# A linear-attention and two-MoE kernel: one visit of each attention step to TensorE from the second block on, and another order inside the slots of the first

## The chip, the cores and the metric

The kernel runs on one core of a Trainium2 chip. The metric is the device time of one execution in microseconds (us). Five engines work side by side, each through its own queue in order: TensorE (PE in the views), VectorE (DVE), ScalarE (ACT), GpSimd (POOL) and SyncE (SP, which here only issues DMAs).

## The reference, cut to what matters

```python
def _attn_ref(q, k, v, f_logit):                 # (4, 8, 768, 48) each
    f = 1.0 / (1.0 + np.exp(-f_logit))
    for t in range(S):
        state = f[:, :, t, :, None] * state + np.einsum('bhd,bhe->bhde', k[:, :, t], v[:, :, t])
        y[:, :, t] = np.einsum('bhd,bhde->bhe', q[:, :, t], state)

x = attention output as (3072, 384)
x = (x @ w_a) * (x @ w_b) @ w_out                # d_ff 1536
h = x @ w_in ; x = (h - np.tanh(h)) @ w_out2     # d_ff 2048
```

## The kernel before

**The attention** is computed in 24 steps: 12 chunks of 64 positions, two batches to a step. Each step is a generator (`attn_step`) that yields between twelve phases, named by letters. F: ACT takes the sigmoid. P and R: DVE scans (tiles PRE and R). K: DVE makes KH and RA (L306, L307). V: ACT copies the running state ST into VS_A and VS_B. S: PE multiplies sc = KH by RA and transposes KH into pk. M: ACT copies RB from RA, then sc into RA and into RB, then pk into KTS (L326 to L333), and POOL masks RA and RB (affine_select, L329). U: PE makes uu from KTS, DVE adds the state into T1 (L348), POOL scales it back into ST. Y: PE makes yy, which reads RA, RB, VS_A and VS_B. E and L: ACT and DVE copy yy into two parts of x. D: DMAs bring a third of the heads into their places.

**The first MoE layer** follows in 6 blocks of 512 tokens, 4 attention steps each. A block has 12 rounds of three groups of nine 128x512 matmuls: a, b, y. Each group is one slot, so a block has 36 slots (`SLOTS`). After a, ACT copies it to asb; after b, DVE multiplies gf = asb times b, ACT makes gh, and gl is the difference (on POOL in block 0, later on DVE). y lags one round. Its sums stay in three PSUM banks for a whole block; after the last y, `store_x2` copies each bank with ACT into oh and subtracts with DVE into ol, and SP stores both. oh and ol have two buffers each for three banks. The steps 0 to 3 run ahead of block 0 by a list written out by hand (`SEQ`); later steps run during the block before the one that needs them. The table `pulses` says at which slot which phase is emitted: in block 0 by FIRST and OFF, later at 9 slots a step. S stands at slot 0 of the nine, U at 2, Y at 3, so a step comes to PE three times.

**The weights** arrive as 64-bit numbers. In block 0 each slot also makes one weight tile (`w_tick`): three DVE operations (cv, cv, wc, L125 to L127), a copy on ACT (L137), a subtraction on POOL (L139). A slot needs about the tile that was made four slots earlier. In block 0 the tick stands ahead of the slot's phases. Later blocks convert the second layer's weights, two tiles in nine slots.

**The second MoE layer** (h and o groups) runs from about 575 us to the end and is not touched.

The order on every queue is the order in which the program emits: `tc.manual_schedule()` moves nothing. `x2` buffers, PSUM banks and staging buffers come free by semaphores.

Of the kernel before, what the change touches and what calls it, by code (L numbers as in the profile page):

```python
# [18 lines left out]
CH = 64  # L19
# [9 lines left out]
def tile_kernel(ctx: ExitStack, tc: tile.TileContext, q, k, v, f, w_a, w_b, w_out, w_in, w_out2, l_fkq, l_tv, l_v, l_w1, l_w2, out):  # L29
    nc = tc.nc  # L30
# [21 lines left out]
    SLOTS = 3 * MF  # L52
    LEAD = 7
    FIRST = (-5, 4, 12, 20)
    PHASES = "FPRKVSMUYELD"
    OFF = (0, 1, 2, 4, 5, 7, 7, 9, 10, 10, 11, 12)
    CONV = (3, 7)
    SEQ = ("lf0 lk0 lf1 lt0 lk1 lv0 lf2 lt1 lv1 lk2 w lf3 lt2 lv2 lk3 w lt3 lv3 w x x x x F0 P0 F1 R0 K0 x x lf4 lk4 x V0 S0 P1 M0 F2 "
# [95 lines left out]
    def bank(i, name):  # L154
        return psp.tile([128, 512], F32, tag=f"b{i}", name=name)
# [3 lines left out]
    def att_bank(name):  # L159
        rot["att"] = (rot["att"] + 1) % rot["n"]  # L160
        return bank(rot["att"], name)

    def mm_split(dst, lhs, rhs, first, last):
        for i, (l_, r_) in enumerate(((lhs[0], rhs[0]), (lhs[0], rhs[1]), (lhs[1], rhs[0]))):
            nc.tensor.matmul(dst, l_, r_, start=(first and i == 0), stop=(last and i == 2))  # L165

    with tc.manual_schedule(), ExitStack() as p1:
# [8 lines left out]
        def gtile(tag, shape, name):  # L176
            bufs = {"gh": 4, "gl": 4, "oh": 2, "ol": 2, "asb": 1}[tag]
            n = 1
            for x in shape[1:]:
                n *= x  # L180
            w = TW if tag in ("gh", "gl") else 512
            t = gp.tile([128, w], F32, tag=tag, name=name, bufs=bufs)[:, :n]
            if len(shape) == 3:
                t = t.rearrange("p (u s) -> p u s", s=shape[2])
            return t

        class Work:
            def __init__(self, mk):
                self.F = mk("gh", [128, TW], "F")
                self.PRE = mk("gh", [128, NS], "PRE")  # L190
                self.R = mk("gl", [128, NS], "R")
                self.D2 = mk("gl", [128, NS], "D2")
                self.VS_A = mk("ol", [128, U, 64], "VS_A")
                self.VS_B = mk("ol", [128, U, 64], "VS_B")
                self.T1 = mk("asb", [128, U, D], "T1")
                self.KH = mk("gh", [128, U, CH], "KH")
                self.RA = mk("gh", [128, U, CH], "RA")
                self.RB = mk("gl", [128, U, CH], "RB")
                self.KTS = mk("gl", [128, 512], "KTS")
                self.F3 = self.F[:, 0:NS].rearrange("p (u s) -> p u s", s=SL)  # L200
                self.PRE3, self.R3, self.D23 = (
                    x.rearrange("p (u s) -> p u s", s=SL) for x in (self.PRE, self.R, self.D2))

        raw = {}
        for name in ("F", "D2", "R", "KH", "KTS", "PRE", "T1", "VX", "VX", "RA", "RB", "VS_A", "VS_B"):
            raw.setdefault(name, []).extend(wpool.tile([128, TW], F32, tag="w", name=name) for _ in range(PRO - 2))
# [12 lines left out]
        for i in range(PRO):  # L219
            work.append(Work((atile, gtile)[i] if i < 2 else wtile))  # L220
        VX = [[wtile("w", [128, 6, 64], "VX") for _ in range(2)] for _ in range(2)]
        VX = [[t.rearrange("p (b k) d -> p b k d", b=2) for t in s_] for s_ in VX]
# [33 lines left out]

        wdum = const.tile([128, 512], BF16, name="wdum")
        nc.vector.memset(wdum, 0.0)
# [23 lines left out]
        def attn_step(i):  # L282
# [19 lines left out]
            yield  # L302
            KH, RA, RB, KTS = w.KH, w.RA, w.RB, w.KTS
            k3 = tk.rearrange("p (u s) -> p u s", s=CH)
# [3 lines left out]
            yield  # L308
            if c > 0:
                nc.scalar.activation(VS_A[0:64, :, 0:D], st[0:64], ACTF.Copy)  # L310
                nc.scalar.activation(VS_B[64:128, :, 0:D], st[64:128], ACTF.Copy)
            if i < PRO:
                for vx, vs in zip(VX[i % 2], (VS_A, VS_B)):
                    nc.scalar.activation(
                        vx[:, :, :, 48:64], vs[:, U - 2:U, 0:D].rearrange("p b (k x) -> p b k x", x=16), ACTF.Copy)
            yield
            sc = att_bank("sc").rearrange("p (u s) -> p u s", s=CH)
            for u in range(U):
                nc.tensor.matmul(sc[64:128, u], KH[0:64, u], RA[0:64, u], start=True, stop=True)  # L319
                nc.tensor.matmul(sc[0:64, u], KH[64:128, u], RA[64:128, u], start=True, stop=True)  # L320
            pk = att_bank("pk")
            for j in range(NJ):
                nc.tensor.transpose(  # L323
                    pk[:, 128 * j:128 * (j + 1)], KH[:, 2 * j:2 * j + 2, :].rearrange("p u s -> p (u s)"), ident)
            yield
            nc.scalar.activation(RB[64:128], RA[64:128], ACTF.Copy)  # L326
            for r_, rows in ((RA, slice(64, 128)), (RB, slice(0, 64))):
# [4 lines left out]
                )  # L332
            nc.scalar.activation(KTS, pk, ACTF.Copy)  # L333
            yield
            uus = [att_bank(f"uu{bl}").rearrange("p (u s) -> p u s", s=CH) for bl in range(2)]
            for j in range(NJ):
# [15 lines left out]
            yield  # L352
            yy = att_bank("yy").rearrange("p (u s) -> p u s", s=CH)
            direct = jb == 0
# [45 lines left out]
        for jb in range(1, NBLK):  # L400
            for si in range(blocks[jb]):
                for p, o in enumerate(OFF):
                    at = FIRST[si] + o if jb == 1 else SLOTS * (jb - 1) + 9 * si - LEAD + o
                    pulses.append((at, first[jb] + si, p))
# [4 lines left out]
        def pulse(i, p):  # L409
            assert phase[i] == p  # L410
            phase[i] += 1
            if i >= PRO and p == 0 and i + 1 < NSTEP:
                load_t(i + 1, slice(0, 3))
            if i >= PRO and PHASES[p] == "K" and i + 1 < NSTEP:
                load_tv(i + 1)
            next(gens[i], None)
            if i >= PRO and PHASES[p] == "Y" and i + 1 < NSTEP:
                load_v(i + 1)
# [27 lines left out]
        def y_group(jb, m):  # L446
            n = 128 * blocks[jb]
            if m == 0:
                ys[jb] = [bank(5 + d, f"y{d}")[:, :n] for d in range(KT)]
            g = G.pop((jb, m))  # L450
            wo = W["o", m]
            for d in range(KT):
                cs = slice(128 * d, 128 * d + 128)
                mm_split(ys[jb][d], [w[:, cs] for w in wo], g, m == 0, m == MF - 1)
            if m == MF - 1:
                store_x2(jb, n)

# [16 lines left out]
        def moe1(prev):  # L474
            for jb in range(NBLK):
                n = 128 * blocks[jb]
                xx = [X[jb][:, hl].rearrange("p k s c -> p k (s c)")[:, :, :n] for hl in range(2)]
                for m in range(MF):
                    pab = []
                    for bi, nm in enumerate("ab"):  # L480
# [6 lines left out]
                        if nm == "a":  # L487
                            asb = gp.tile([128, 512], F32, tag="asb", name="asb", bufs=1)[:, :n]
                            nc.scalar.activation(asb, pb, ACTF.Copy)  # L489
                            yield jb  # L490
                    gf = gp.tile([128, 512], F32, tag="gf", name="gf", bufs=1)[:, :n]
                    gh = gp.tile([128, TW], F32R, tag="gh", name="gh", bufs=4)[:, :n]
# [15 lines left out]
        for it in SEQ.split():  # L508
            if it == "c":
                w_tick(nconv[0] + 1)  # L510
            elif it == "w":
                w_fetch(len(loaded) + 1)
            elif it == "x":
                warm()
            elif it[0] == "l":
                i = int(it[2])
                if it[1] == "f":
                    load_t(i, slice(0, 1))
                elif it[1] == "k":
                    load_t(i, slice(1, 3))  # L520
                else:
                    (load_tv if it[1] == "t" else load_v)(i)
            else:
                i, p = int(it[1]), PHASES.index(it[0])
                if i >= PRO:
                    pulses.pop(0)
                pulse(i, p)
        for i in range(PRO):
            pulse(i, len(PHASES) - 1)
        npro = nconv[0]  # L530
# [13 lines left out]
        for g, jb in enumerate(moe1(None)):  # L544
            slot = g % SLOTS
            if jb == 0:
                w_tick(min(NW1, npro + slot + 1))
            else:
                if g == SLOTS:
                    rot.update(n=3, conv=None)  # L550
                if spilled:
                    w_spill()
                if (g + LEAD) % (SLOTS // 4) in CONV and jb < NBLK - 1 or (jb == NBLK - 1 and slot == 0):
                    w_tick(min(nconv[0] + 1, NW2 + 1))
# [249 lines left out]
```

## Time and profile before

| | |
|---|---|
| median of 3 runs | 980.62 us (980.6 to 981.83) |
| the profiled execution | 981.35 us, span 979.4 us |
| PE busy | 952.7 us, 97% of the span |
| DVE busy | 605.5 us, 62% |
| ACT busy | 491.4 us, 50% |
| POOL busy | 133.4 us, 14% |

The span runs from the first to the last instruction; the execution's own time is 1.95 us longer and 0.73 us above the median. Matmuls overlap, and their ends are modelled, so the distance from one start to the next tells more than a busy share. The views give in brackets how long an instruction's engine sat idle before it and what ended that.

### The profile page before, as it was taken

The page shows a single profiled execution, that of the slowest core. Times are in us where ns is not written, and L with a number is a line of the kernel's source. Part 1 is how long each engine was busy: PE and PEld are TensorE (multiplying, and loading weights), DVE is VectorE, ACT ScalarE, POOL GpSimd, SP SyncE. Part 2 cuts the span into 40 slices and gives each one's busy share as a digit, 9 for nine tenths or more (in the row PEclk, how much of TensorE's full clock was granted, in tenths as well). Part 3 has the DMA queues.
Part 4 walks back from the last instruction along what each step waited for, and adds up shares of the span by engine and source line. Part 5 has one row for each costly group of instructions (what it writes and reads, how often), then busy time and mean ns, then how long its engine had stood idle before and what let it go on. Part 6 is the DMA issues. An engine that isn't in the chain of part 4 may idle for free.

```text
span 979.4 us, 15868 instructions
## 1 busy us (share of the span) xinstructions
PE 952.7 (97%) x6155; PEld 766.7 (78%) x6155; DVE 605.5 (62%) x1021; ACT 491.4 (50%) x949; POOL 133.4 (14%) x144
## 2 busy tenths in 40 slices
PE   7898899999999999999999999999999999999997
PEld 5677777878888878877888888888888888888885
DVE  6988866556666665565442257666666666666663
ACT  5544544344433444443321156666666666666663
POOL 6566651111111111111000000000000000000000
PEclk9999999999999999999999999999999999999999
DMA  9566656445534643472248650100100100200001
GB/s 284 134 185 172 185 125 192 113 108 179 145 108 125 195 124 109 141 196 85 76 159 291 192 180 1 63 35 1 65 33 1 65 33 16 82 0 1 33 1 35
DMA packets 41171, 104.53 MB, mean 107 GB/s; under 512 B 5600, under 2 KB 8672, under 8 KB 41088
## 3 DMA queue, kind: packets, MB, share of 16 engines
q1 hardware_dynamic: 40368, 102.45, 35.3%
q10 hardware_dynamic: 720, 0.98, 0.5%
q8 instruction: 50, 0.82, 0.4%
q14 instruction: 33, 0.27, 0.1%
HBM read 74.71 MB, written 26.74 MB: 104 GB/s over the span
## 4 chain that ended last, share of the span: by engine, by line
PE 88%; DVE 6%; issue 2%; ACT 2%; DMA 1%; SPq 0%; POOL 0%; DVEq 0%; ACTq 0%
PE o L165 20%; PE h L165 20%; PE b L165 14%; PE a L165 13%; PE y L165 13%; PE yy L358 2%; PE sc L319 2%; DVE cv L126 2%; PE uu L340 1%; DVE cv L125 1%; PE pk L323 1%; DVE wc L127 1%; DMA VS_B<-in_l_v_dram 1%; DVE R L299 1%; DVE gf L494 0%
## 5 line engine op out<-in xcount | busy, mean ns | idle before, releaser
L165 PE MATMUL h<-x,w_i 128*128 128x512 f32 x864 | 212.6, 391 | 0.0
L165 PE MATMUL o<-gh,w_p 128*128 128x512 f32 x576 | 195.1, 394 | 0.0
L165 PEld LDWEIGHTS h<-x,w_i 128*128 128x128 f32 x864 | 162.2, 188 | 36.1
L165 PE MATMUL a<-x,w_a 128*128 128x512 f32 x648 | 163.9, 397 | 2.6 <-ACT asb L489 2.3
L165 PE MATMUL b<-x,w_b 128*128 128x512 f32 x648 | 164.4, 398 | 0.0
L165 PE MATMUL y<-gh,w_o 128*128 128x512 f32 x432 | 148.0, 397 | 0.0
L165 PEld LDWEIGHTS a<-x,w_a 128*128 128x128 f32 x648 | 120.3, 188 | 30.4 <-ACT asb L489 2.7
L165 PEld LDWEIGHTS b<-x,w_b 128*128 128x128 f32 x648 | 119.9, 189 | 25.3
L105 DVE SCALAR_TENSOR_TENSOR xu<-u,h 128x512 f32<-128x512 f32 x96 | 66.0, 688 | 111.4 <-ACT u L102 111.2
L494 DVE TENSOR_TENSOR gf<-asb,b 128x512 f32<-128x512 f32 x72 | 49.3, 685 | 137.2 <-PE b L165 84.6
L165 PEld LDWEIGHTS o<-gh,w_p 128*128 128x128 f32 x576 | 108.1, 188 | 25.0 <-issue 0.2
L102 ACT ACTIVATE u<-h 128x512 f32<-128x512 f32 x96 | 57.4, 598 | 132.6 <-PE h L165 131.9
L165 PE MATMUL o<-gl,w_p 128*128 128x512 f32 x288 | 112.9, 392 | 0.0
L495 ACT ACTIVATE gh<-gf 128x512 fp32r<-128x512 f32 x72 | 45.5, 632 | 130.7 <-DVE gf L494 130.6
L489 ACT ACTIVATE asb<-a 128x512 f32<-128x512 f32 x72 | 42.9, 596 | 132.1 <-PE a L165 130.5
L165 PEld LDWEIGHTS y<-gh,w_o 128*128 128x128 f32 x432 | 81.8, 189 | 18.9
L165 PE MATMUL y<-gl,w_o 128*128 128x512 f32 x216 | 85.4, 395 | 0.0
L107 DVE SCALAR_TENSOR_TENSOR v<-v,v 128x512 f32<-128x512 f32 x96 | 66.5, 693 | 10.3 <-ACT gh L575 0.5
L106 DVE SCALAR_TENSOR_TENSOR v<-v,xu 128x512 f32<-128x512 f32 x96 | 66.5, 692 | 10.3 <-ACT v L103 0.5
L103 ACT ACTIVATE v<-u,bias 128x512 f32<-128x512 f32 x96 | 69.5, 724 | 3.1
L104 ACT ACTIVATE v<-u,bias 128x512 f32<-128x512 f32 x96 | 68.1, 709 | 0.6 <-DVE gl L576 0.6
L576 DVE TENSOR_TENSOR gl<-v,gh 128x512 fp32r<-128x512 f32 x96 | 65.7, 685 | 0.2 <-ACT gh L575 0.2
(95 smaller groups left out, 1114.4 us busy)
## 6 DMA issues: line engine op xcount, KB each, us to landing
wst<-in_l_w_dram SPq DMA_DIRECT2D x68, 384.0 KB, 3.3
wsp<-wst SPq DMA_DIRECT2D x32, 384.0 KB, 2.6
T<-in_l_fkq_dram SPq DMA_DIRECT2D x38, 288.0 KB, 5.4
x<-xs SPq DMA_DIRECT2D x12, 768.0 KB, 5.2
w_i<-wsp SPq DMA_DIRECT2D x16, 384.0 KB, 3.5
w_p<-wsp SPq DMA_DIRECT2D x16, 384.0 KB, 3.5
TV<-in_l_tv_dram SPq DMA_DIRECT2D x24, 192.0 KB, 2.8
xs<-oh SPq DMA_DIRECT2D x18, 256.0 KB, 2.3
```

The costliest lines, as they stand in the source:

```text
L102: nc.scalar.activation(u, h, ACTF.Square, accum_out=total)
L103: nc.scalar.activation(v1, u, ACTF.Square, bias=bias1)
L104: nc.scalar.activation(v2, u, ACTF.Square, bias=bias2)
L105: nc.vector.scalar_tensor_tensor(xu, u, Q4, h, ALU.mult, ALU.mult)
L106: nc.vector.scalar_tensor_tensor(v1, v1, Q_Y1, xu, ALU.add, ALU.mult)
L107: nc.vector.scalar_tensor_tensor(v2, v2, Q_Y2, v1, ALU.add, ALU.mult)
L126: nc.vector.scalar_tensor_tensor(t, hi, -1073741824, t, ALU.bitwise_and, ALU.bitwise_or)
L165: nc.tensor.matmul(dst, l_, r_, start=(first and i == 0), stop=(last and i == 2))
L489: nc.scalar.activation(asb, pb, ACTF.Copy)
L494: nc.vector.tensor_tensor(gf, asb, pab[1], ALU.mult)
L495: nc.scalar.activation(gh, gf, ACTF.Copy)
L576: nc.vector.tensor_tensor(gl, g, gh.bitcast(F32), ALU.subtract)
```

## The change

From step 8 on (`ONE`), the table of slots is a new one: for each step the slot sv of S and M, and yv of U, Y and E, where yv of a step is sv of the next. PE so gets uu and yy of one step and sc and pk of the next one behind each other, at slots 2, 11, 20 and 29 of a block (2, 11, 17, 23, 29 in block 1). Five fixed banks are used for this: uu takes the two banks of a and b (3 and 4). RA and RB get a second pair, since yy now reads them after the next step's are made. V moves behind M. Loads of TV are issued from U, two steps ahead. In all steps, those ahead of block 0 too, KTS is copied first in M. In block 0 the slot's phases are emitted ahead of the slot's weight tile. `store_x2` is emitted at slot 3 of the next block, ahead of which it stood at slot 2, directly behind the last y and ahead of that slot's phases. Some buffers are shared: T1 lies in R, gf lies in asb from block 1 on and in oh's two buffers in block 0.

```diff
-    FIRST = (-5, 4, 12, 20)
-    OFF = (0, 1, 2, 4, 5, 7, 7, 9, 10, 10, 11, 12)
-    CONV = (3, 7)
+    PHASES = "FPRKVSMUYELD", "FPRKSMVUYELD"
+    ONE = first[2]
...
+    for j in range(2, NBLK):
+        at = (2, 11, 17, 23, 29) if j == 2 else (-7, 2, 11, 20, 29)
+        for si in range(4):
+            sv, yv = (SLOTS * (j - 1) + at[x] for x in (si, si + 1))
+            pre = (7, 6, 4, 2) if j < 3 else (8, 7, 5, 2)
+            VISIT[first[j] + si] = tuple(sv - o for o in pre) + (sv, sv, sv + 1, yv, yv, yv, yv + 1, yv + 2)
+    CONV = (5, 8)
...
+    def step_bank(i, name):
+        if i < ONE:
+            return att_bank(name)
+        return bank({"uu0": 3, "uu1": 4, "yy": 0, "sc": 1, "pk": 2}[name], name)
...
-                self.T1 = mk("asb", [128, U, D], "T1")
+                self.T1 = self.R[:, 0:U * D].rearrange("p (u d) -> p u d", d=D)
...
+            nc.scalar.activation(KTS, pk, ACTF.Copy)
             nc.scalar.activation(RB[64:128], RA[64:128], ACTF.Copy)
...
-            nc.scalar.activation(KTS, pk, ACTF.Copy)
...
             if m == MF - 1:
-                store_x2(jb, n)
+                ready.append((jb, n))
...
-                    gf = gp.tile([128, 512], F32, tag="gf", name="gf", bufs=1)[:, :n]
+                    gf = asb if jb > 0 else gp.tile([128, 512], F32, tag="oh", name="gf", bufs=2)
...
             slot = g % SLOTS
+            if ready and slot > 2:
+                store_x2(*ready.pop(0))
             if jb == 0:
+                while pulses and pulses[0][0] <= g:
+                    _, i, p = pulses.pop(0)
+                    pulse(i, p)
                 w_tick(min(NW1, npro + slot + 1))
```

ACT in block 0, from round 0's gh to round 1's: step 4's M stands here. Before:

```order
L495 ACTIVATE gh<-gf 128x512
L137 ACTIVATE w_o_727<-wc 128x384
L137 ACTIVATE w_a_737<-wc 128x384
L326 ACTIVATE RB<-RA 64x512
L328 ACTIVATE RA<-sc 64x512
L328 ACTIVATE RB<-sc 64x512
L333 ACTIVATE KTS<-pk 128x512
L489 ACTIVATE asb<-a 128x512
```

Of the change, at the same place:

```order
L520 ACTIVATE gh<-gf 128x512
L144 ACTIVATE w_o_725<-wc 128x384
L344 ACTIVATE KTS<-pk 128x512
L345 ACTIVATE RB<-RA 64x512
L347 ACTIVATE RA<-sc 64x512
L347 ACTIVATE RB<-sc 64x512
L144 ACTIVATE w_a_763<-wc 128x384
L514 ACTIVATE asb<-a 128x512
```

KTS moves from behind the three copies to their front, and the weight tile w_a moves from their front to behind them.

PE in block 3, where one step's uu ends and its yy begins (w_a is round 4's weight). Before:

```order
L340 MATMUL uu_3859<-TV_183,KTS 64x48 x2
L340 MATMUL uu_3860<-TV_183,KTS 64x48 x2
L165 MATMUL a<-x,w_a_955 128x512 x9
L358 MATMUL yy<-RA,VS_A 64x64
L358 MATMUL yy<-RB,VS_B 64x64
```

Of the change, in the same block, from the end of uu and, behind the dots of yy, to the next group a:

```order
L361 MATMUL uu_3829<-TV_181,KTS 64x48 x2
L361 MATMUL uu_3830<-TV_181,KTS 64x48 x2
L379 MATMUL yy<-RA_odd,VS_A 64x64
L379 MATMUL yy<-RB_odd,VS_B 64x64
...
L379 MATMUL yy<-RA_odd,VS_A 64x64
L379 MATMUL yy<-RB_odd,VS_B 64x64
L337 MATMUL sc<-RA,KH 64x64
L338 MATMUL sc<-RA,KH 64x64
...
L341 MATMUL pk<-ident,KH 128x128 x4
L177 MATMUL a<-x,w_a_956 128x512 x9
```

The group a that stood between uu and yy is gone from there, and sc and pk of the next step follow on yy (its sixteen matmuls, and sc's, alternate as the rows shown).

ACT where block 1 has ended and block 2 begins (y is the old block's bank, asb and gh are round 1 of the new one). Before:

```order
L333 ACTIVATE KTS<-pk 128x512
L495 ACTIVATE gh<-gf 128x512
L463 ACTIVATE oh<-y_1960 128x512
L463 ACTIVATE oh<-y_1961 128x512
L463 ACTIVATE oh<-y_1962 128x512
L292 ACTIVATE F<-T_182 128x8x64
L489 ACTIVATE asb<-a 128x512
```

Of the change:

```order
L344 ACTIVATE KTS<-pk 128x512
L345 ACTIVATE RB_odd<-RA_odd 64x512
L347 ACTIVATE RA_odd<-sc 64x512
L347 ACTIVATE RB_odd<-sc 64x512
L514 ACTIVATE asb<-a 128x512
L488 ACTIVATE oh<-y_1900 128x512
L488 ACTIVATE oh<-y_1901 128x512
L488 ACTIVATE oh<-y_1902 128x512
L326 ACTIVATE VS_A<-ST_131 64x8x48
L327 ACTIVATE VS_B<-ST_131 64x8x48
L306 ACTIVATE F<-T_178 128x8x64
L520 ACTIVATE gh<-asb 128x512
```

The three oh copies move from ahead of asb to behind it, and so behind the whole visit; the new block's first y still follows round 1's b on PE.

## Rows read from the trace of the kernel before

**Rows 1.** Stretches: us, busy us (instructions) of PE, weight loads, DVE, ACT, POOL; clock; DMA.

```profile
35.60:139.40 103.80, 91.49 (x716) 72.56 (x716) 89.67 (x161) 48.09 (x94) 64.12 (x59) 0.97 0.67 176
139.40:150.00 10.60, 10.60 (x97) 8.26 (x98) 4.52 (x7) 6.03 (x11) 2.60 (x3) 0.84 0.03 9
139.40:571.00 431.60, 431.60 (x3211) 347.32 (x3212) 228.45 (x417) 166.07 (x310) 47.44 (x49) 1.00 0.50 147
```

**Rows 2.** PE's waits up to 150 us: total, times, longest, in us.

```profile
PE uu L340 <- ACT KTS L333: 12.0, 7, 3.0
...
PE a L165 <- ACT asb L489: 2.3, 1, 2.3
```

**Rows 3.** DVE's waits from 35.6 to 139.4 us.

```profile
DVE gf L494 <- ACT asb L489: 3.7, 3, 1.7
DVE gf L494 <- PE b L165: 3.2, 2, 1.9
DVE gf L494 <- POOL w_o L139: 1.6, 1, 1.6
```

**Rows 4.** ACT in order of time at step 4's M: start, length, operation.

```profile
47.45 0.63 ACT L326 ACTIVATE RB<-RA 64x512 f32<-64x512 f32 x1
...
49.22 0.58 ACT L333 ACTIVATE KTS<-pk 128x512 f32<-128x512 f32 x1
49.70 0.58 ACT L489 ACTIVATE asb<-a 128x512 f32<-128x512 f32 x1
```

**Rows 5.** DVE in order of time at the end of block 0.

```profile
132.40 1.72 DVE L299 TENSOR_TENSOR_SCAN R<-F,D 128x520 f32<-128x520 f32 x1
...
136.35 0.68 DVE L307 TENSOR_TENSOR RA<-T,PRE 128x512 f32<-128x512 f32 x1
```

**Rows 6.** ACT in order of time, step 2's M, ahead of block 0.

```profile
23.60 0.63 ACT L326 ACTIVATE RB<-RA 64x512 f32<-64x512 f32 x1
...
25.63 0.58 ACT L333 ACTIVATE KTS<-pk 128x512 f32<-128x512 f32 x1
```

**Rows 7.** POOL in order of time, the same step.

```profile
26.35 0.99 POOL L329 TENSOR_SCALAR_AFFINE_SELECT RB<-RB 64x512 f32<-64x512 f32 x1
```

**Rows 8.** PE in order of time, the same step.

```profile
24.34 0.66 PE L323 MATMUL pk<-ident,KH 128*128 128x128 f32 x4
...
26.26 0.68 PE L340 MATMUL uu<-TV,KTS 64*64 64x48 f32 x32 [1.05 <-ACT KTS L333]
```

**Rows 9.** PE in order of time, block 2 and the end of block 4.

```profile
299.77 0.27 PE L319 MATMUL sc<-RA,KH 64*64 64x64 f32 x1
...
301.26 2.32 PE L165 MATMUL b<-x,w_b 128*128 128x512 f32 x9
...
305.55 0.68 PE L340 MATMUL uu<-TV,KTS 64*64 64x48 f32 x32
306.17 2.34 PE L165 MATMUL a<-x,w_a 128*128 128x512 f32 x9
...
308.43 0.27 PE L358 MATMUL yy<-RA,VS_A 128*64 128x64 f32 x1
...
309.51 2.34 PE L165 MATMUL b<-x,w_b 128*128 128x512 f32 x9
...
492.80 2.22 PE L165 MATMUL a<-x,w_a 128*128 128x512 f32 x9
494.86 0.39 PE L165 MATMUL b<-x,w_b 128*128 128x512 f32 x1
```

**Rows 10.** ACT in order of time, the store after block 0.

```profile
148.35 1.07 ACT L463 ACTIVATE oh<-y 128x512 fp32r<-128x512 f32 x2
151.09 0.60 ACT L463 ACTIVATE oh<-y 128x512 fp32r<-128x512 f32 x1 [1.68 <-DMA xs<-oh]
```

**Rows 11.** DVE in order of time, the same store.

```profile
149.08 1.28 DVE L464 TENSOR_TENSOR ol<-y,oh 128x512 fp32r<-128x512 f32 x2
151.93 0.69 DVE L464 TENSOR_TENSOR ol<-y,oh 128x512 fp32r<-128x512 f32 x1 [1.56 <-DMA xs<-ol]
```

More of the change, by code (lines that the diff above doesn't have):

```diff
@@ L52, in tile_kernel @@
     SLOTS = 3 * MF
-    LEAD = 7
-    FIRST = (-5, 4, 12, 20)
-    PHASES = "FPRKVSMUYELD"
-    OFF = (0, 1, 2, 4, 5, 7, 7, 9, 10, 10, 11, 12)
-    CONV = (3, 7)
+    PHASES = "FPRKVSMUYELD", "FPRKSMVUYELD"
+    ONE = first[2]
+    VISIT = {}
+    for si, at in enumerate((-5, 4, 12, 20)):
+        VISIT[PRO + si] = tuple(at + o for o in (0, 1, 2, 4, 5, 7, 7, 9, 10, 10, 11, 12))
+    for j in range(2, NBLK):
[5 more added lines that the diff above has]
+    CONV = (5, 8)
     SEQ = ("lf0 lk0 lf1 lt0 lk1 lv0 lf2 lt1 lv1 lk2 w lf3 lt2 lv2 lk3 w lt3 lv3 w x x x x F0 P0 F1 R0 K0 x x lf4 lk4 x V0 S0 P1 M0 F2 "
@@ L176, in gtile @@
         def gtile(tag, shape, name):
-            bufs = {"gh": 4, "gl": 4, "oh": 2, "ol": 2, "asb": 1}[tag]
+            bufs = {"gh": 4, "gl": 4, "oh": 2, "ol": 2}[tag]
             n = 1
@@ L204, in tile_kernel @@
         raw = {}
-        for name in ("F", "D2", "R", "KH", "KTS", "PRE", "T1", "VX", "VX", "RA", "RB", "VS_A", "VS_B"):
+        for name in ("F", "D2", "R", "KH", "KTS", "PRE", "VX", "VX", "RA", "RB", "VS_A", "VS_B"):
             raw.setdefault(name, []).extend(wpool.tile([128, TW], F32, tag="w", name=name) for _ in range(PRO - 2))
@@ L220, in tile_kernel @@
             work.append(Work((atile, gtile)[i] if i < 2 else wtile))
+        RAB = [(work[0].RA, work[0].RB),
+               tuple(ap.tile([128, U, CH], F32, name=nm) for nm in ("RA_odd", "RB_odd"))]
         VX = [[wtile("w", [128, 6, 64], "VX") for _ in range(2)] for _ in range(2)]
@@ L255, in load_tv @@
             nc.sync.dma_start(out=tv_of(i), in_=l_tv[i])
-        wdum = const.tile([128, 512], BF16, name="wdum")
+        wdum = wpool.tile([128, 256], F32, tag="w", name="wdum").bitcast(BF16)
         nc.vector.memset(wdum, 0.0)
@@ L302, in attn_step @@
             yield
-            KH, RA, RB, KTS = w.KH, w.RA, w.RB, w.KTS
+            KH, KTS = w.KH, w.KTS
+            RA, RB = (w.RA, w.RB) if i < ONE else RAB[i % 2]
             k3 = tk.rearrange("p (u s) -> p u s", s=CH)
@@ L308, in attn_step, with copy_state @@
             yield
[L309 to L317, printed above, removed]
+            def copy_state():
+                if c > 0:
+                    nc.scalar.activation(VS_A[0:64, :, 0:D], st[0:64], ACTF.Copy)
+                    nc.scalar.activation(VS_B[64:128, :, 0:D], st[64:128], ACTF.Copy)
+                if i < PRO:
+                    for vx, vs in zip(VX[i % 2], (VS_A, VS_B)):
+                        nc.scalar.activation(
+                            vx[:, :, :, 48:64], vs[:, U - 2:U, 0:D].rearrange("p b (k x) -> p b k x", x=16), ACTF.Copy)
+            if i < ONE:
+                copy_state()
+                yield
+            sc = step_bank(i, "sc").rearrange("p (u s) -> p u s", s=CH)
             for u in range(U):
@@ L320, in attn_step @@
                 nc.tensor.matmul(sc[0:64, u], KH[64:128, u], RA[64:128, u], start=True, stop=True)
-            pk = att_bank("pk")
+            pk = step_bank(i, "pk")
             for j in range(NJ):
@@ L332, in attn_step @@
                 )
-            nc.scalar.activation(KTS, pk, ACTF.Copy)
             yield
-            uus = [att_bank(f"uu{bl}").rearrange("p (u s) -> p u s", s=CH) for bl in range(2)]
+            if i >= ONE:
+                copy_state()
+                yield
+            uus = [step_bank(i, f"uu{bl}").rearrange("p (u s) -> p u s", s=CH) for bl in range(2)]
             for j in range(NJ):
@@ L352, in attn_step @@
             yield
-            yy = att_bank("yy").rearrange("p (u s) -> p u s", s=CH)
+            yy = step_bank(i, "yy").rearrange("p (u s) -> p u s", s=CH)
             direct = jb == 0
@@ L401, in tile_kernel @@
             for si in range(blocks[jb]):
-                for p, o in enumerate(OFF):
-                    at = FIRST[si] + o if jb == 1 else SLOTS * (jb - 1) + 9 * si - LEAD + o
+                for p, at in enumerate(VISIT[first[jb] + si]):
                     pulses.append((at, first[jb] + si, p))
@@ L411, in pulse @@
             phase[i] += 1
-            if i >= PRO and p == 0 and i + 1 < NSTEP:
+            ph = PHASES[i >= ONE][p]
+            if i >= PRO and ph == "F" and i + 1 < NSTEP:
                 load_t(i + 1, slice(0, 3))
-            if i >= PRO and PHASES[p] == "K" and i + 1 < NSTEP:
+            if PRO <= i <= ONE and ph == "K":
                 load_tv(i + 1)
             next(gens[i], None)
-            if i >= PRO and PHASES[p] == "Y" and i + 1 < NSTEP:
+            if i >= ONE and ph == "U" and i + 2 < NSTEP:
+                load_tv(i + 2)
+            if i >= PRO and ph == "Y" and i + 1 < NSTEP:
                 load_v(i + 1)
@@ L455, in y_group @@
             if m == MF - 1:
-                store_x2(jb, n)
+                ready.append((jb, n))
+        ready = []
         def store_x2(jb, n):
@@ L523, in tile_kernel @@
             else:
-                i, p = int(it[1]), PHASES.index(it[0])
+                i, p = int(it[1]), PHASES[0].index(it[0])
                 if i >= PRO:
@@ L528, in tile_kernel @@
         for i in range(PRO):
-            pulse(i, len(PHASES) - 1)
+            pulse(i, len(PHASES[0]) - 1)
         npro = nconv[0]
@@ L552, in tile_kernel @@
                     w_spill()
-                if (g + LEAD) % (SLOTS // 4) in CONV and jb < NBLK - 1 or (jb == NBLK - 1 and slot == 0):
+                if g % (SLOTS // 4) in CONV and jb < NBLK - 1 or (jb == NBLK - 1 and slot == 0):
                     w_tick(min(nconv[0] + 1, NW2 + 1))
@@ L566, in tile_kernel @@
                     w_fill(*fills.pop(0))
+        store_x2(*ready.pop(0))
         pa.close()
```

## The prediction

> **What bounds the kernel now.** I read the stretches first. From 139.4 us to 571 us TensorE is busy for 431.60 us of 431.60 [rows 1], so in blocks 1 to 5 nothing else than TensorE's own instructions makes up the time: an edit there counts only if it takes work from TensorE or makes it wait. Block 0 is different. In its 103.8 us, from 35.6 to 139.4, TensorE is busy for 91.49 and VectorE for 89.67 [rows 1], and neither is full. There I read whom each waits for. TensorE's largest wait is uu for KTS, 12.0 us in 7 pieces (a few of them ahead of block 0), and one a group waits 2.3 us [rows 2]. VectorE waits 3.7, 3.2 and 1.6 us in gf, for asb, b and w_o [rows 3]; so the two wait for each other in turn, with ScalarE's queue between them: step 4's KTS starts at 49.22, behind three copies that began at 47.45, and asb stands behind it at 49.70 [rows 4]. The third place is the time ahead of block 0, where step 2's uu waits 1.05 us for KTS [rows 8] while POOL masks RB only from 26.35 [rows 7].
>
> The sum is made against the profiled execution, 981.35 us, that is 1.95 us more than its span; the median shown is 0.73 us less, so the forecast is 0.73 below the sum.
>
> **Ahead of block 0: +5.0 us (2 to 6.5).** KTS first costs here, though it was made for uu. KTS needs pk, which ends at 24.34 + 0.66 = 25.00 [rows 8]. Before, RB's copy of RA (23.60) ran while TensorE still made sc and pk, and KTS at 25.63 followed RB's copy of sc [rows 6]. Now all four begin at 25.00, and four copies take 2.25 us (47.45 to 49.70, [rows 4]): they end at 27.25. RB's copy of sc, that was done at about 25.7, ends up to 27.25 - 25.63 = 1.6 us later, and POOL's mask of RB, 0.99 us behind it [rows 7], with it. yy reads the masked RB, and the next step's sc stands behind yy on TensorE. TensorE's own work does not cover it: before, uu from 26.26 to 26.94 was followed by the mask's end at 27.34. I take 1.25 us for each of four steps: nearer to 1.6 than to 0.5, which is what would stay if the conversions of weights between the phases covered most of a mask. Four times 0.5 and 1.6 are the bounds.
>
> **Block 0: -12.1 us (-4 to -17).** Removed are the waits of uu: KTS starts at once, three copies (49.22 - 47.45 = 1.77 us) earlier, and the weight tile's copy is no longer ahead of it either, about 2.3 us together. None of uu's waits is longer than 3.0 [rows 2]. Not all that time is TensorE's to win, since VectorE's chain has to shrink with it. VectorE's 103.8 lose its waits for asb, b and the weight w_o, 3.7 + 3.2 + 1.6 = 8.5 us [rows 3]. Step 8's R and K leave the end of the block: 1.72 + 2 x 0.68 [rows 5] and two small operations, 3.4 us. 103.8 - 8.5 - 3.4 = 91.9 us is VectorE's floor. TensorE's is its 91.49 less some 3.4 us, since its granted clock was 0.97 of the higher level [rows 1] and 0.03 of 103.8 us went there, so 88. I take 92.5, that is 11.3 us less, and 0.8 more since the clock of 0.84 behind the block's last wait [rows 1] cost 0.16 x 10.6 = 1.7 us, and the shorter wait ahead of it should give half back. The low bound is the a group's 2.3 us and the clock's 1.7; the high one is 12.0 + 2.3 of waits and 3.4 of clock, less a little for the steps ahead of the block. What is against it: phases ahead of the weight tile make each tile later by that slot's scans and products, up to 1.72 us or 1.36 us [rows 5], and a tile is needed four slots on.
>
> **Visits: -6.2 us (-3.1 to -6.7).** Blocks 1 to 5 had 3 x 16 = 48 visits; now there are 17, so 31 are gone. The small matmuls stay. What a visit costs beyond them: the group a between uu and yy takes 308.43 - 306.17 = 2.26 us from start to start, an undisturbed one 494.86 - 492.80 = 2.06 [rows 9]. So 0.20 us each, 31 x 0.20 = 6.2. The high end is 0.215 a visit, as far as the hundredths of such starts go; the low end belongs to a rival.
>
> **The store: +9.4 us (0 to 14).** Five times the old block's three y banks have to be copied before the new block's y groups can write them. Before, oh began at 148.35, and the last ol ended at 151.93 + 0.69 = 152.62 [rows 10, 11]. There are two oh and two ol buffers, so the third copy waits for the first one's DMA: 148.35 to 151.09, with one copy of 0.6 within it, is 2.16 us from the first copy's end, and ol the same, 149.77 to 151.93 [rows 10, 11]. This was hidden: y could not start before a, b and the old block's y and again a and b. Now `store_x2` stands at slot 3, so ScalarE has KTS, three copies and asb ahead of oh. Count from the start of the slot-2 visit. It takes 0.62 (uu, 306.17 - 305.55) + 1.08 (yy, 309.51 - 308.43) + 1.49 (sc and pk, 301.26 - 299.77) = 3.19 us [rows 9]; then a and b, 2.26 + 2.06: y wants its first bank at 7.4 and its third at 8.8. KTS starts when pk ends, near 3.2, four copies and asb make it 5.8, oh is done with its first bank at 6.4, ol at 7.0; the third oh starts 2.16 later, and the third ol, behind it and behind its own buffer, ends near 10.6. TensorE waits 1.8 to 1.95 us for y's third bank, five times: 9.4. If ScalarE gets to asb a copy earlier and the DMAs land sooner it is 0; if ol waits for a DMA that has to queue behind the spilled weights, 2.8 each, 14.
>
> **Costed at nothing.** T1 in R, so the next R waits for POOL's ST: TensorE's next visit is nine slots off, and VectorE has half of its time free in blocks 1 to 5 (228.45 busy of 431.60, [rows 1]). gf in asb: the next asb waits for gl, and a y group of 2 us lies between. Fixed banks 3 and 4 for uu: T1's two additions have to end before a and b write there; sc, pk and yy, 2.57 us [rows 9], lie between. Without that cover each would cost up to 0.7 us a visit. The second RA and RB pair and earlier TV loads take no engine's time.
>
> Sum: 5.0 - 12.1 - 6.2 + 9.4 = -3.9, so 977.45 profiled and 976.7 by the median. Less than 0.2% (2 us) is about what a measurement cannot tell from no change.
>
> **The rivals.**
> - *The store stays hidden* (0.15): y's third bank is free in time, since oh's DMA lands sooner than 2.16 us or asb comes earlier. For it: 1.8 us is only three copies of 0.6 [rows 10]. Against it: both third pieces waited for their buffers in the trace [rows 10, 11]. -13.3, so 967.3.
> - *The time ahead of block 0 stays* (0.10): weight conversions fill ScalarE there anyway. Against it: uu's wait for KTS was visible [rows 8], so ScalarE was the one waited for. -8.9, so 971.7.
> - *Shapes, not visits, cost* (0.12): the rows carry the shape of the array: sc and uu are 64x64, yy is 128x64, pk and the groups 128x128 [rows 8, 9]. Before, three visits made six changes of shape in a step. One visit has four left (to uu, to yy, to sc, to pk). If 0.20 is two changes, 0.10 each, the step keeps 0.40 of 0.60, and 31 x 0.10 = 3.1 us are saved. Sum -0.8, so 979.8. [...] No row here has two small shapes alone behind each other, so the trace does not decide it; the visits of three shapes will.
> - *Block 0 is bound by weight tiles* (0.23), the other side: with the phases ahead, cv and wc of a tile come 1.4 to 1.7 us later in slots with R or K [rows 5], TensorE waits at a, b or y for its weight in place of uu for KTS, and VectorE's queue stays the chain. If only the low bound's 4 us are left, the sum is 5.0 - 4 - 6.2 + 9.4 = +4.2, so 984.8. It is slower than before by over 2 us from a gain below 6.2.
>
> **How the numbers follow.** The forecast has 0.40; its own range, with half a bound off in one term, is 973 to 981. The likeliest is 976.7. Below 969.5 lies the store's rival for the most part (0.13), above 984.5 half of the last one (0.10 or a little less). Faster by over 0.2%: 0.33 of the forecast's 0.40, 0.15 and 0.10, so 0.58. Within: 0.05 of the forecast, 0.11 of the shapes, 0.04 of the tiles: 0.20. Slower: 0.02, 0.01 and 0.19, so 0.22.
>
> **What the profile of the changed kernel would show.** Ahead of block 0: its first a at about 40.6 in place of 35.6, with yy waiting for POOL's RB. In block 0: no wait of uu for KTS over 1 us, block 1's first a near 133; a wait of a, b or y for w would be the last rival. In blocks 1 to 5: 17 visits, and a lone 2.26 us group ahead of each instead of three; the visit itself no longer than the sum of its parts, 3.19. The store: TensorE's y waits for ol about 1.8 us, five times. The forecast is wrong above all if those five waits are missing, or if block 0 gains what one bound says instead of the middle.

## The result, and the profile after

The changed kernel takes 986.56 us (median, 985.46 to 990.01) against 981.96 us before (980.6 to 982.53): 4.6 us between the two medians. The ratio on record, which is not the quotient of these two medians (1.0047), is 1.0065 with a 95% interval of 1.0053 to 1.0076, so about 6 us. The change made the kernel slower, where 976.7 was forecast, and the time lies above the range. Its profiled execution has a span of 986.4 us, 7.0 more than before.

Where the 7.0 us lie is read from the stretches of the changed kernel, cut at the first a of block 0, the first a of block 1 and the end of block 5 (columns as in [rows 1]):

```profile
0.00:42.80 42.80, 30.59 (x482) 21.57 (x482) 25.24 (x49) 21.52 (x44) 19.00 (x37) 0.96 0.76 203
42.80:144.66 101.86, 92.33 (x716) 70.41 (x716) 93.15 (x160) 47.42 (x94) 62.39 (x58) 0.98 0.64 171
144.66:582.10 437.44, 429.95 (x3230) 351.07 (x3229) 234.16 (x424) 170.06 (x313) 37.63 (x49) 1.00 0.50 146
```

Ahead of block 0 the kernel takes 42.8 us in place of 35.6. Block 0 takes 101.9 in place of 103.8 [rows 1]: 1.9 less, and not 11.3. VectorE does more work in it (93.15 us, it was 89.67), though R and K of step 8 are gone from there. Blocks 1 to 5 take 437.4 us; before, they took 436.0 (139.37 to 575.40). TensorE, that had no gap there, now waits 7.5 us. The rest of the span is 0.3 us longer.

TensorE's waits in the changed kernel (total, times, longest; beside [rows 2]):

```profile
PE y L177 <- DVE ol L489: 7.2, 9, 1.6
PE uu L361 <- ACT RB L347: 4.4, 4, 1.8
PE yy L379 <- POOL RA L348: 4.0, 4, 1.4
PE sc L337 <- DVE RA L322: 4.0, 1, 4.0
PE uu L361 <- ACT KTS L344: 1.6, 3, 0.7
```

Three of them matter. yy waits for POOL's mask ahead of block 0, as forecast. y waits for ol, as forecast. But uu in block 0 waits for RB, a tile that uu does not read.

**Ahead of block 0.** In order of time, step 2's M in the changed kernel, which answers to [rows 6 to 8]:

```profile
29.44 0.66 PE L341 MATMUL pk<-ident,KH 128*128 128x128 f32 x4
...
30.13 0.60 ACT L344 ACTIVATE KTS<-pk 128x512 f32<-128x512 f32 x1 [1.49 <-PE pk L341]
30.75 0.63 ACT L345 ACTIVATE RB<-RA 64x512 f32<-64x512 f32 x1
30.78 0.68 PE L361 MATMUL uu<-TV,KTS 64*64 64x48 f32 x32 [0.47 <-ACT KTS L344]
...
31.41 0.59 ACT L347 ACTIVATE RA<-sc 64x512 f32<-64x512 f32 x1
...
32.03 0.59 ACT L347 ACTIVATE RB<-sc 64x512 f32<-64x512 f32 x1
32.13 0.66 POOL L348 TENSOR_SCALAR_AFFINE_SELECT RA<-RA 64x512 f32<-64x512 f32 x1 [6.03 <-ACT RA L347]
...
32.84 0.33 PE L379 MATMUL yy<-RA,VS_A 128*64 128x64 f32 x2 [1.38 <-POOL RA L348]
```

All four copies stand behind pk. uu comes 0.6 us sooner after pk's start (1.34 us against 26.26 - 24.34 = 1.92, [rows 8]), and yy 0.9 us later (3.40 against 26.87 - 24.34 = 2.53). uu's gain is worth nothing, since yy follows it.

**Block 0.** In order of time, step 6 in the changed kernel, and step 7's scan behind its uu:

```profile
104.04 0.58 ACT L344 ACTIVATE KTS<-pk 128x512 f32<-128x512 f32 x1
...
105.92 0.59 ACT L347 ACTIVATE RB<-sc 64x512 f32<-64x512 f32 x1
...
106.57 0.68 PE L361 MATMUL uu<-TV,KTS 64*64 64x48 f32 x32 [1.83 <-ACT RB L347]
...
107.37 1.02 POOL L146 TENSOR_TENSOR w_o<-wc,w_o 128x384 fp32r<-128x384 f32 x1
...
107.82 3.42 DVE L308 TENSOR_TENSOR_SCAN PRE<-F,D 128x520 f32<-128x520 f32 x1
...
108.34 1.01 POOL L146 TENSOR_TENSOR w_a<-wc,w_a 128x384 fp32r<-128x384 f32 x1
109.31 0.83 POOL L372 TENSOR_TENSOR ST<-R,PMS 128x384 f32<-128x384 f32 x1
```

KTS is done at 104.62, and uu starts at 106.57, when the last copy of sc has ended: 2 us after its input. And a PRE scan, which takes 1.23 us at its shortest, takes 3.42 us here. POOL runs three operations without a gap in that time, and the scan ends 1.1 us after the last of them.

**The store.** In order of time, block 1's store at the head of block 2 (beside [rows 10, 11]):

```profile
248.12 0.59 ACT L347 ACTIVATE RB_odd<-sc 64x512 f32<-64x512 f32 x1
...
249.10 1.07 ACT L488 ACTIVATE oh<-y 128x512 fp32r<-128x512 f32 x2
...
251.86 0.60 ACT L488 ACTIVATE oh<-y 128x512 fp32r<-128x512 f32 x1 [1.69 <-DMA xs<-oh]
...
252.97 0.69 DVE L489 TENSOR_TENSOR ol<-y,oh 128x512 fp32r<-128x512 f32 x1 [1.96 <-DMA xs<-ol]
...
253.71 0.50 PE L177 MATMUL y<-gh,w_o 128*128 128x512 f32 x1 [1.58 <-DVE ol L489]
```

The third ol waits 1.96 us for a DMA and ends at 253.66, and y's third bank starts at 253.71. This is the forecast chain, at the head of five blocks. The third bank's waits are 1.20 to 1.58 us, 6.5 in all; in four of the blocks the second bank waits 0.17 us too.

### The profile page after: what moved, and what is told of

It reads as the page before. It is cut to its first block, busy times and chain, and to the rows that moved or that the text cites. A ratio compares the mean times of both kernels' runs of the same rounds, so it can differ in the third digit from the quotient of the medians.

```text
span 986.4 us, 15901 instructions
## 1 busy us (share of the span) xinstructions
PE 949.6 (96%) x6155; PEld 767.1 (78%) x6155; DVE 611.3 (62%) x1021; ACT 493.4 (50%) x949; POOL 119.0 (12%) x144
## 4 chain that ended last, share of the span: by engine, by line
PE 83%; DVE 7%; ACT 4%; DMA 2%; issue 2%; POOL 1%; DVEq 0%; SPq 0%; ACTq 0%; POOLq 0%
PE o L177 20%; PE h L177 20%; PE y L177 12%; PE a L177 12%; PE b L177 12%; PE yy L379 2%; PE sc L337 2%; DVE cv L133 1%; PE uu L361 1%; PE pk L341 1%; DMA xs<-ol 1%; DVE cv L132 1%; DVE PRE L308 1%; DMA T<-in_l_fkq_dram 1%; DVE R L313 1%
## 5 line engine op out<-in xcount | busy, mean ns | idle before, releaser
L177 PE MATMUL b<-x,w_b 128*128 128x512 f32 x648 | 160.1, 391 | 1.9 <-DVE gf L519 1.3
L519 DVE TENSOR_TENSOR asb<-asb,b 128x512 f32<-128x512 f32 x60 | 41.1, 686 | 113.4 <-PE b L177 112.9
L177 PEld LDWEIGHTS y<-gh,w_o 128*128 128x128 f32 x432 | 80.8, 188 | 32.4 <-DVE ol L489 11.3
L520 ACT ACTIVATE gh<-asb 128x512 fp32r<-128x512 f32 x60 | 37.9, 632 | 108.3 <-DVE asb L519 108.3
```

What stands on the lines that cost most here:

```text
L519: nc.vector.tensor_tensor(gf, asb, pab[1], ALU.mult)
L520: nc.scalar.activation(gh, gf, ACTF.Copy)
```

## The experiments

All times are medians in us. Before took 981.96 beside the changed kernel, and 980.43, 979.99 and 980.08 beside the three sets below, so the ratios to before are compared; a difference in us below is one of medians, and by the ratios it is up to about 1 us smaller or larger. "First a" and "block 0" are read from the traces: when a begins in block 0, and how long until it begins in block 1.

| kernel | time | ratio to before, 95% | first a | block 0 | blocks 1 to 5 |
|---|---|---|---|---|---|
| before | | 1 | 35.61 | 103.76 | 436.03 |
| the change | 986.56 | 1.0065 (1.0053 to 1.0076) | 42.80 | 101.86 | 437.44 |
| KTS last ahead of block 0 | 980.87 | 1.0017 (1.0006 to 1.0028) | 35.92 | 100.57 | 437.94 |
| store as before | 981.90 | 1.0019 (1.0008 to 1.0031) | 42.30 | 101.83 | 432.51 |
| block 0 as before | 992.32 | 1.0121 (1.0100 to 1.0142) | 43.11 | 104.68 | 440.21 |
| all three | 978.15 | 0.9974 (0.9961 to 0.9987) | 35.24 | 102.94 | 433.79 |
| KTS last in block 0 | 982.80 | 1.0036 (1.0021 to 1.0051) | 40.31 | 98.84 | 437.40 |
| tile ahead in block 0 | 991.42 | 1.0114 (1.0095 to 1.0132) | 42.03 | 103.41 | 442.19 |
| P behind the tile | 983.01 | 1.0031 (1.0020 to 1.0043) | 41.94 | 98.43 | 437.09 |
| uu in a's bank | 985.89 | 1.0060 (1.0042 to 1.0077) | 41.01 | 102.50 | 437.77 |
| store in two parts | 976.00 | 0.9958 (0.9944 to 0.9973) | 40.43 | 101.87 | 426.89 |
| three repairs | 967.33 | 0.9865 (0.9848 to 0.9883) | 36.48 | 97.27 | 427.40 |
| three repairs, KTS last in block 0 | 967.30 | 0.9866 (0.9847 to 0.9884) | 35.89 | 96.94 | 428.04 |

**KTS last ahead of block 0.** For the steps 0 to 3 the copy goes back behind the masks:

```diff
-            nc.scalar.activation(KTS, pk, ACTF.Copy)
+            if not (i < PRO):
+                nc.scalar.activation(KTS, pk, ACTF.Copy)
...
+            if (i < PRO):
+                nc.scalar.activation(KTS, pk, ACTF.Copy)
```

> The changed kernel with KTS last again in the four steps ahead of block 0 alone. Theory (the four copies now begin only when pk ends, so POOL's masks of RA and RB and with them yy and the next step's sc come later): first a back from 42.8 us to about 36, yy's wait for POOL's RA (4.0 us in 4) gone, and 986.6 - 6.5 = 980 us, 979 to 981. Rival (the 7.2 us come from a later start of the first step and from the lower clock there): less than 3 us come back, 984 or more.

It took 980.87, 5.7 us less than the changed kernel, and the first a is back at 35.92. TensorE's waits up to then:

```profile
PE uu L364 <- ACT KTS L354: 3.9, 3, 1.6
...
PE yy L382 <- POOL RB L349: 0.2, 1, 0.2
```

uu waits for KTS again (3.9 us, 1.6 with the change), and yy no longer for POOL. The longer wait of uu is the cheaper one, since it ends while the masks run. The theory holds.

**The store as before.** `store_x2` again stands where the last y is emitted:

```diff
-                ready.append((jb, n))
+                store_x2(jb, n)
...
-            if ready and slot > 2:
-                store_x2(*ready.pop(0))
```

> The changed kernel with the store of x2 directly behind the last y again, ahead of the slot-2 visit. Theory (y waits for the third bank since three copies of the visit and asb stand ahead of oh on ScalarE): y's waits for ol, 7.2 us in 9, go, and 986.6 - 7 = 979.5 us, 978.5 to 981. Rival (the store's three copies ahead of the visit's only move the wait: KTS, the copies of sc and asb come 1.8 us later and a, b or uu wait for them): at most 3 us come back, 983.5 or more.

981.90: 4.7 us came back, between the two. y's waits are gone, but a has 3.3 us of waits in blocks 1 to 5 that neither kernel had. In order of time, with block 2's store:

```profile
330.76 0.66 PE L341 MATMUL pk<-ident,KH 128*128 128x128 f32 x4
...
332.64 0.69 DVE L487 TENSOR_TENSOR ol<-y,oh 128x512 fp32r<-128x512 f32 x1 [3.28 <-DMA xs<-ol]
...
333.25 0.61 DVE L369 TENSOR_TENSOR R<-uu,ST 128x192 f32<-128x192 f32 x2
...
333.65 0.73 PE L177 MATMUL a<-x,w_a 128*128 128x512 f32 x2 [2.23 <-DVE R L369]
```

T1's additions (they write R now) stand on VectorE behind the third ol, which waits for its buffer's DMA, and a cannot write the bank of uu until they have read it. So theory and rival were both partly right: the stall moved. That the fixed banks cost nothing holds only while no waiting ol stands ahead of T1.

**Block 0 as before.** Steps 4 to 7 with KTS last, and the weight tile ahead of the slot's phases:

```diff
             if jb == 0:
-                while pulses and pulses[0][0] <= g:
-                    _, i, p = pulses.pop(0)
-                    pulse(i, p)
                 w_tick(min(NW1, npro + slot + 1))
```

> The changed kernel with steps 4 to 7 in block 0 as before: KTS last, weight tile ahead of the slot's phases. Theory (uu takes sc's bank of the two that rotate in block 0, so it waits for the last copy of sc whatever the place of KTS; the order of the slots brings little): block 0 is 101 to 104 us against 101.9, so the time is 985 to 988.5. Rival A (phases ahead of the tile make tiles late and cost several us): 982 to 984. Rival B (the order did bring what was forecast and something else took it): over 991.

992.32, 5.8 us more, so my theory fell and the time is rival B's: the new order does bring something, and something else takes it. uu waits 9.6 us for KTS here, 4.4 with the change. But block 0 itself is only 2.8 us longer than with the change (104.68 against 101.86). Blocks 1 to 5, where the two kernels do the same, are 2.8 us longer too. Most of that is block 3 (92.0 us against 89.6): behind a wait of y for ol of 2.0 us the granted clock was 0.50 for 3.4 us.

**All three together**, which leaves the visits and the shared buffers.

> The changed kernel with all three of these edits, so that of the change only the visits from the second block on and the shared buffers are left. Theory (31 visits fewer are worth 5 to 6 us, R and K of step 8 have left block 0, and nothing waits): 986.6 - 6.5 - 7 + 1 = 974 us, 972 to 977, faster than before by about 8. Rival (shapes, not visits, cost, so half of it): 977 to 980. If waits at the visits come with the early store: 981 or more.

978.15, faster than before by 0.26%. That is the first rival's time and not for its reason: a waits 3.6 us for T1 at the store, as above, and uu 9.1 us for KTS in block 0. The visits are a gain, and the early store spoils part of it.

**KTS last in block 0**, the first diff with `PRO <= i < ONE`; **the tile ahead**, the third diff alone; **P behind the tile**:

```diff
-                while pulses and pulses[0][0] <= g:
+                while pulses and pulses[0][0] <= g and pulses[0][2] != 1:
```

and **uu in a's bank**:

```diff
     def step_bank(i, name):
+        if name == "uu0" and PRO <= i < ONE:
+            rot["att"] = (rot["att"] + 1) % rot["n"]
+            return bank(3, name)
```

> The changed kernel with KTS last again in steps 4 to 7 alone; their phases stay ahead of the weight tile. Theory (in block 0 uu is written to sc's bank, of two that rotate, and so waits for the last copy of sc; all four copies are needed in either order): uu waits as long as now, 4.4 us in 4, block 0 stays at 101.9 us within 1, and the time at 986.6 within 1.5. Rival (uu waits for KTS alone, so its place is what shortened the wait): four times up to 1.8 us more, block 0 at 105 to 109 and the time at 990 or more.

> The changed kernel with the weight tile ahead of the slot's phases again in block 0, and KTS still first. Theory (what shortened uu's wait is the order inside the slot, which moves M's copies ahead of the tile's copy; what ate it are the PRE scans that now run beside POOL): uu waits 9 to 12 us in block 0 as before, PRE is back at 1.2 to 1.4 us, and as KTS's place does nothing the time is that of the run with both undone, 990 to 994. Rival (KTS first is what helps): 984 to 987.

> The changed kernel with, in block 0, P (the PRE scan) and what follows it in its slot behind the weight tile, all other phases ahead of it as in the change. Theory (PRE takes up to 3.4 us as POOL's ST, w_o and w_a run beside it, and VectorE is what block 0 waits for): PRE's mean falls from 2.5 to about 1.4 us and block 0 from 101.9 to 97 to 99, so 982 to 984.5. Rival (PRE's length is hidden, since uu's waits for the copies of sc set the end): block 0 within 1 us, 985.5 to 988.

> The changed kernel with the first half of uu of steps 4 to 7 in a's bank, and so the second half in pk's, instead of sc's and pk's. Theory (sc's bank is what keeps uu waiting behind KTS): uu's wait for RB (4.4 us in 4) falls below 1 us; the time gains what VectorE lets through, 2 to 4 us: 982.5 to 985. Rival A (uu waits for KTS itself or for the masks all the same): no change, 986 to 988. Rival B (a then waits for T1's additions, which read a's bank): slower, 988 or more.

uu's waits in block 0 (total, times, longest; 4.4 with the change): with KTS last, with the tile ahead, with both (block 0 as before), and with uu in a's bank, in this order:

```profile
PE uu L364 <- ACT KTS L354: 3.6, 3, 1.8
PE uu L361 <- ACT RB L347: 8.6, 4, 3.1
PE uu L364 <- ACT KTS L354: 9.6, 4, 3.0
PE uu L364 <- ACT asb L517: 7.2, 3, 2.6
```

With KTS last in block 0, uu waits 3.6 us, no longer than the changed kernel's 4.4; so KTS's place does not shorten the wait, as the theory said. But the time fell by 3.8 us (2.8 by the ratios), which it did not say. The group of VectorE's PRE scans from 45 to 130 us (steps 5 to 7; total, mean) tells where that comes from, first in the changed kernel:

```profile
L308 DVE TENSOR_TENSOR_SCAN PRE<-F,D 128x520 f32<-128x520 f32 x3 | 8.4, 2801 | 0.0
```

with KTS last in block 0:

```profile
L308 DVE TENSOR_TENSOR_SCAN PRE<-F,D 128x520 f32<-128x520 f32 x3 | 5.3, 1780 | 0.0
```

with P behind the tile:

```profile
L308 DVE TENSOR_TENSOR_SCAN PRE<-F,D 128x520 f32<-128x520 f32 x3 | 4.4, 1463 | 0.0
```

The scans are 3.1 and 4.0 us shorter, and block 0 is 3.0 and 3.4 us shorter. So with the tile behind the phases, block 0 follows the scans almost us for us: VectorE is what it waits for. The granted clock does not explain it: over the profiled execution it was 0.995 with the change, and 0.995 and 0.992 in these. P behind the tile took 983.01, 3.6 us less, as expected. In its trace the scan starts as POOL's w_o ends, and now it is POOL's next operation that is long:

```profile
60.35 1.01 POOL L146 TENSOR_TENSOR w_o<-wc,w_o 128x384 fp32r<-128x384 f32 x1
...
61.28 1.23 DVE L308 TENSOR_TENSOR_SCAN PRE<-F,D 128x520 f32<-128x520 f32 x1
...
62.00 1.32 POOL L146 TENSOR_TENSOR w_a<-wc,w_a 128x384 fp32r<-128x384 f32 x1 [0.64 <-ACT w_a L144]
```

With the tile ahead and KTS first, the scans take 4.3 us, and uu waits 8.6 us (9.6 with KTS last): 991.42 and 992.32 are the same within their intervals. So it is the place of the tile that shortens uu's wait, by about half, and not the place of KTS. What that place is worth in time is less clear: block 0 is 1.5 and 2.8 us longer with the tile ahead, and blocks 1 to 5, 4.8 and 2.8 us longer, come out of the same program text as the change's. Why KTS's place makes the scans longer in one order is not tested; that POOL's masks and tiles come at other moments is an argument only.

With uu in a's bank uu no longer waits for RB but 7.2 us for asb, which has to leave that bank first, and the time is the same as the change's. That sc's bank is what held uu is therefore shown by what uu waits for (RB, which it does not read, and in a's bank the copy that reads a), and by the order of KTS that does not matter; no run here had a free bank for it.

**The store in two parts**: two banks directly behind the last y, the third at slot 3:

```diff
-                ready.append((jb, n))
+                store_x2(jb, n, range(2))
+                ready.append((jb, n, range(2, KT)))
...
-            for d in range(KT):
+            for d in ds:
```

> The changed kernel with the store in two parts: two of the three y banks directly behind the last y, as before, the third at slot 3, behind the visit. Theory (y waits for its second and third bank since the store stands behind the visit, and with all three ahead of it T1's additions stand behind the third ol, which waits for a DMA, and a waits for T1): neither wait stays, 986.6 - 9 = 977.5 us, 976 to 979.5. Rival (the third ol still holds up T1, y or asb): 2 us or more of waits for ol or R stay in blocks 1 to 5, 980 or more.

976.00, and TensorE has no wait in blocks 1 to 5. The stretch from the first a of block 1 to the end of block 5:

```profile
142.30:569.19 426.89, 426.89 (x3231) 351.86 (x3230) 233.62 (x424) 169.28 (x313) 37.63 (x49) 1.00 0.51 150
```

It is 10.6 us shorter than with the change.

**Three repairs**, with KTS first in block 0 and with KTS last there.

> Three repairs together: KTS last ahead of block 0, P behind the weight tile in block 0, and the store in two parts. Theory (the three costs lie in different stretches, so they add): 986.6 - 6 - 3.5 - 9 = 968 us, 966 to 971, about 12 faster than before. Rival (a shorter stretch ahead of block 0 or in it is lost again to waits for weights or to the clock): 972 or more.

> The same three repairs, and KTS last in block 0 too, so nowhere first before step 8. Theory (uu of steps 4 to 7 waits for all four copies in either order, and with P behind the tile PRE no longer collides with POOL in either): the same as the three repairs within 1.5 us. Rival (KTS last is better by itself, as its 3 us in the run with KTS last in block 0 alone): 965 or less.

967.33 and 967.30, 0.9865 of before (0.9848 to 0.9883). Alone the repairs gave 5.7, 3.6 and 10.6 us, 19.9 together; the three at once gave 19.2 (by the ratios 18.5 and 19.6). With P behind the tile, KTS's place in block 0 makes no difference. The stretches of the first of the two:

```profile
0.00:36.48 36.48, 27.61 (x483) 19.34 (x483) 26.59 (x52) 21.17 (x44) 20.75 (x37) 1.00 0.82 228
36.48:133.75 97.27, 90.98 (x715) 70.86 (x716) 88.98 (x158) 47.97 (x94) 62.32 (x60) 0.98 0.67 182
133.75:561.15 427.40, 427.40 (x3231) 352.01 (x3229) 232.91 (x423) 168.95 (x312) 37.40 (x49) 1.00 0.51 150
```

## Why the prediction was wrong

| term | forecast | measured in the profiled runs |
|---|---|---|
| ahead of block 0 | +5.0 (2 to 6.5) | +7.2 |
| block 0 and the clock behind it | -12.1 (-4 to -17) | -1.9 - 1.6 = -3.5 |
| visits | -6.2 (-3.1 to -6.7) | -7.5 |
| store | +9.4 (0 to 14) | +10.6 |
| rest of the span | 0 | +0.3 |
| sum | -3.9 | +7.1 (span +7.0) |

**The step that failed is block 0**: "Removed are the waits of uu: KTS starts at once", and behind it the floor of 91.9 us for VectorE. By the sum of the prediction that floor is 86.3 us of work and 5.6 of waiting; measured were 93.15 and 8.7. Two things were wrong in it.

First, uu does not wait for KTS alone. In block 0 two PSUM banks rotate among sc, pk, uu and yy (`rot.update(n=2, conv=2)`), so the first half of uu takes sc's bank and needs both copies of sc to be done. Ahead of block 0 six rotate, and there uu does start behind KTS. I took the wait's name in [rows 2], "uu <- ACT KTS", for its cause: KTS was the last of four copies that uu needed anyway. With the phases ahead of the tile all four start sooner, so the wait halves, to 4.4 us; it does not go. Nor do VectorE's waits in gf, which were to lose all of their 8.5 us: 3.2 are left.

Second, VectorE's work was taken as fixed. 3.1 us (R, KH and RA of step 8) did leave the block, and yet its busy time rose by 3.5 us: the three PRE scans of steps 5 to 7 take 8.4 us instead of 3.8, and 1.4 us of steps 3 and 4 (T1's additions and the end of a scan) now lie behind the block's first a. The rest is for the most part R, KH and RA of the other steps, which became longer as well. I had priced a scan ahead of a tile at its usual duration (the tile is late by as much), and not asked what POOL does in that moment. Ahead of the tile, PRE starts where POOL still has ST and weight tiles to do; behind it, POOL is nearly done with them. In the changed kernel PRE took 1.23 us alone (at 203.81 us) and 3.42 us beside 2.3 us of POOL's. The conversions cv and wc stay at 0.53 to 0.56 us in block 0 before and after, beside POOL or not. Why the scan becomes longer there and they do not, no run here shows.

The rival that came nearest is the last, in size (984.8), in that block 0 hardly gains and in that VectorE's queue stays the chain. Its tiles are the smaller part: TensorE waits 2.5 us for w_a, w_b and w_o in block 0, in pieces of 0.3 to 0.9, and 4.4 for the copies that uu needs. And the tiles are late by the long scans more than by the new order: with KTS last in block 0, where the phases still stand ahead of the tile and the scans are 3.1 us shorter, TensorE waits 1.0 us for them. Even the shortest block 0 here, 96.9 us, is above the 92.5 of the forecast; uu's wait, 5.2 us there, is the largest that is left. (A slip that moved nothing: 0.03 of 103.8 us is 3.1, not 3.4.)

**Ahead of block 0** the mechanism was right and the size 2.2 us low. Steps 0, 2 and 3 each became 1.0 to 1.2 us longer from sc to sc, as forecast (1.25). Step 1 became 2.8 us longer: the granted clock of this stretch is 0.96, and it was 0.50 from 24.5 to 27.9 us, where its yy took 3.4 us, and 2.0 before. In the run with the store in two parts, which has the same program text ahead of block 0, it became 1.0 us longer. 1.1 us more is a later first sc (9.67 against 8.56); in the other kernels here with KTS first it was 8.56 to 9.11, so that part is mostly this run's. In eight kernels with KTS first the first a came between 40.31 and 43.11 us, in four with KTS last at 35.24 to 36.48.

**The visits** gave more than forecast. A block with four visits in place of twelve, without stalls, takes 87.58 us (block 2, store in two parts) and took 89.51: 1.93 us for 8, so 0.24 each, and 31 x 0.24 = 7.5. The forecast's 0.20 was low because the row it took for an undisturbed group, 2.06, is a little long: without visits near it a group takes 2.04, and the four groups between uu and yy in block 2 before take 2.26 to 2.29. The visit itself takes 3.19 us, as worked out. The rival on shapes, which would have left half, falls: the inner changes of shape, uu to yy to sc to pk, show no price.

**The store** behaved as worked out in its mechanism: y's third bank starts where the third ol ends, in each of five blocks. That 10.6 us came so near to 9.4 is partly luck. By [rows 10, 11] the third ol ends 152.62 - 148.35 = 4.27 us after the first oh begins, so at 5.8 + 4.27 = 10.1 and not 10.6; the waits are then 1.3 each, 6.4 in all, which is what the third bank did wait (6.5). What was left out made up for it: the second bank's 0.7 us, and 3.1 us for which the views call TensorE busy (429.95 us with the change, 426.89 with the store in two parts), since its matmuls stand further apart at a wait (in block 2 the first behind a wait starts 0.33 or 0.34 us ahead of the next, and other matmuls of y there 0.23). In block 2 it is 8.58 us from the a behind the first visit to the next a (245.94 to 254.52), and with the store in two parts 6.23 (241.00 to 247.23): 2.35 more, of which 1.75 are waits. What the prediction lacked is that the store's old place was not safe either once the visits had moved there.

That nothing else would cost anything held in blocks 1 to 5: with the store in two parts no wait is left there.

## What to carry to other kernels

A wait carries the name of the last thing that came, not of all that are needed: before moving that one forward, list what else the waiting instruction needs, its output's bank included. When work is moved to another place in a queue, ask what the other engines do at that moment, not only what stands in the queue: a scan on VectorE that costs 1.2 us in one place cost 3.4 in another. And a stall that is repaired by moving it forward may stand ahead of something else; here two banks could be stored early and the third could not.

## What the hardware showed that was not expected

In two meetings of a scan with an operation of POOL, both shown above, the one at work first kept its length and the other became longer. PRE that starts while POOL runs w_o took 3.42 us (1.23 alone), and POOL's w_o and w_a kept their 1.0 us; PRE that starts ahead of POOL's w_a took 1.23 us, and w_a took 1.32. But the first start is not all that decides. With KTS last in block 0, step 7's PRE starts in w_o as well, w_a follows w_o without a gap, and yet here it is w_a that pays. In order of time:

```profile
103.57 1.01 POOL L146 TENSOR_TENSOR w_o<-wc,w_o 128x384 fp32r<-128x384 f32 x1
...
104.18 1.50 DVE L308 TENSOR_TENSOR_SCAN PRE<-F,D 128x520 f32<-128x520 f32 x1
...
104.54 1.94 POOL L146 TENSOR_TENSOR w_a<-wc,w_a 128x384 fp32r<-128x384 f32 x1
```

What decides which of the two becomes longer, the scan or POOL's next operation, no run here shows.

The granted clock behind block 0's end was 0.84 in the 10.6 us after a 2.3 us wait [rows 1, 2], and without that wait, in the changed kernel, 1.00 for the whole stretch; so about 1.6 us of block 1 came back with the wait (436.0 - 426.9 with the store in two parts, less 7.5 for the visits), twice the 0.8 of the forecast.
